# Two-step or three-pass value in the first chunk, weight copies shared out, and an earlier read-back, in a Fourier mixing and GEGLU kernel

## The chip, the cores and the metric

The kernel runs on one core of one Trainium2 chip. The metric is the device time of one execution in microseconds (us); less is better. Nearly all numbers below come from one profiled execution of each kernel, read with the whole program's start as time zero.

TensorE, VectorE, ScalarE and GpSimd are written PE, DVE, ACT and POOL in the profile; PEld is the loading of matmul weights, SP the sync engine that issues most DMAs.

## The reference

```python
X = np.fft.fft(np.fft.fft(x, axis=1), axis=2).real     # x: 8 x 3008 x 256, float32
t = X.reshape(8 * 3008, 256)
g, val = t @ w_gate, t @ w_val                         # 256 x 1536 each
out = (gelu(g) * val) @ w_out                          # 1536 x 256; erf form of gelu
```

## The kernel before

The Fourier transform over the sequence is done by matmuls per batch; the one over the 256 channels is folded into the gate and value weights, which the kernel makes at its start (`make_w`). By symmetry a row and its mirror share an even part E and an odd part O: the gate of a row is E + O, and that of its mirror is E - O with a correction for one channel. The kernel makes a third gate weight "M" (O times -2, one channel set to 0), so that the mirror's gate is a third pass that adds to the same PSUM tile.

The value has no third pass before the change. Its mirror is worked out on VectorE as 2 x VE - V, and the product with the mirror's gelu runs on GpSimd:

```python
def l1_value(ci, fc):
    def run():
        n, c0, E, O, st, fs = cols_of(ci, fc)
        pv = psum("v")
        mm(pv, n, "v", "E", fs, E, True, True)
        ve = ve_tile()
        nc.vector.scalar_tensor_tensor(               # VE: even part plus one channel's term
            ve[:, :n], EB_bufs[b][:, c0 : c0 + n], yw[:, fc : fc + 1], pv[:, :n],
            op0=ALU.mult, op1=ALU.add)
        st["ps"][fc] += [pv, ve]
    return run

def l1_value2(ci, fc):
    def run():
        n, _, _, O, st, fs = cols_of(ci, fc)
        _, gl, pv, ve = st["ps"].pop(fc)
        mm(pv, n, "v", "O", fs, O, False, True, skip_group_check=True)
        nc.vector.tensor_tensor(st["h"][:, fc, 0, :n], gl[:, 0, :n], pv[:, :n], op=ALU.mult)
        vv = v_tile()
        nc.vector.scalar_tensor_tensor(
            _sub(vv, [[-1, n]], n - 1), ve[:, :n], 2.0, pv[:, :n], op0=ALU.mult, op1=ALU.subtract)
        nc.gpsimd.tensor_tensor(st["h"][:, fc, 1, :n], gl[:, 1, :n], vv[:, :n], op=ALU.mult)
    return run
```

Work is laid out in 288 slots, one for each of 12 blocks of 128 features in each of 24 chunks. A slot has a block's gate and value matmuls, the second half of the block before, output matmuls of the chunk before, and "fill" work from a plan:

```python
parts["G"][fc]()                      # gate: E and O passes, first gelu
if before: before[0]["g"][before[1]]()    # third gate pass of the block before, second gelu
parts["V"][fc]()                      # value
...                                   # output matmuls of the chunk before
if before: before[0]["v"][before[1]]()    # value, second part, of the block before
for f in fill.pop(i, []): f()         # weights, transforms of the next batch, ...
```

From the third batch on, the transformed rows S go to DRAM and come back in another layout as Z. The plan puts the two writes (12 and 4 groups of columns) and the read like this, where `s` is the slot of the last transform:

```python
if i == 2: at(fill, s + 1, z_write(b, 0, 12))
if i == 3: at(fill, s + 1, z_write(b, 12, 4))
...
at(fill, s + 3, z_read(b))            # sync engine: Z_sb <- z
...
spread(b, items, s + 7, s0 + NS - 3)  # transposes that read Z_sb, the first at s + 7
```

The stores of the output go through the same sync engine, in program order with these.

Of the kernel before, what the change touches and what calls it, by code (L numbers as in the profile page):

```python
# [28 lines left out]
def kernel(  # L29
# [110 lines left out]
    def psum(tag):  # L140
        bufs = {"g": 2, "v": 3, "o": 1, "dft": 2}[tag]
        return psum_pool.tile([128, 512], FP32, tag=tag, bufs=bufs, name=f"ps_{tag}")
# [283 lines left out]
    def load_wo(q):  # L426
# [3 lines left out]
            in_=ap_replace(  # L430
                moe_w_out, ap=[[C, 128], [128 * C, n], [1, C]], offset=moe_w_out.offset + q * n * 128 * C))

    def make_w(i, f0, n, parts=(0, 1), engine="A", m_at=None, tag="dft"):

        def run():
            ps = psum(tag)
            for k, part in enumerate(parts):
                for half in range(2):
                    nc.tensor.matmul(
                        ps[:, k * n : (k + 1) * n], CW[:, part, half, :], w_raw[:, i, half, f0 : f0 + n],  # L440
                        start=half == 0, stop=half == 1)
            m = n * len(parts)
            dst = _sub(W_sb, [[F, len(parts)], [1, n]], (2 * i + parts[0]) * F + f0)
            if engine == "A":
                nc.scalar.activation(dst, ps[:, :m], AF.Copy)  # L445
            else:
                nc.vector.tensor_copy(dst, ps[:, :m])
            if i == 0 and 1 in parts:
                def minus():
                    nc.scalar.activation(W["g", "M"][:, f0 : f0 + n], ps[:, m - n : m], AF.Copy, scale=keep2)  # L450

                if m_at is None:
                    minus()
                else:
                    m_at.append(minus)
        return run
# [189 lines left out]
    def ffn_work(b):  # L646
        cstate = {}

        def mm(ps, n, nm, part, fs, src, start, stop, **kw):
            nc.tensor.matmul(ps[:, :n], W[nm, part][:, fs], src, start=start, stop=stop, **kw)  # L650

        def cols_of(ci, fc):
            n, c0 = chunk_len[ci], chunk_off[ci]
            E, O = (EO_bufs[b][:, i, c0 : c0 + n] for i in range(2))
            if ci not in cstate:
                cstate[ci] = {"h": h_tile(), "ps": {}, "pso": {}}
            return n, c0, E, O, cstate[ci], slice(fc * 128, (fc + 1) * 128)

        def l1_gate(ci, fc):
            def run():  # L660
                n, _, E, O, st, fs = cols_of(ci, fc)
                pg = psum("g")
                mm(pg, n, "g", "E", fs, E, True, False)
                mm(pg, n, "g", "O", fs, O, False, True)
                gl = gelu_tile()
                nc.scalar.activation(gl[:, 0, :n], pg[:, :n], AF.Gelu)  # L666
                st["ps"][fc] = [pg, gl]
            return run

        def l1_gate2(ci, fc):  # L670
            def run():
                n, _, _, O, st, fs = cols_of(ci, fc)
                pg, gl = st["ps"][fc][:2]
                mm(pg, n, "g", "M", fs, O, False, True, skip_group_check=True)
                nc.scalar.activation(_sub(gl, [[-1, n]], TOK + n - 1), pg[:, :n], AF.Gelu)  # L675
            return run

        def l1_value(ci, fc):
            def run():
                n, c0, E, O, st, fs = cols_of(ci, fc)  # L680
                pv = psum("v")
                mm(pv, n, "v", "E", fs, E, True, True)
                ve = ve_tile()
                nc.vector.scalar_tensor_tensor(  # L684
# [6 lines that stand above are left out]
            def run():  # L691
                n, _, _, O, st, fs = cols_of(ci, fc)
                _, gl, pv, ve = st["ps"].pop(fc)
                mm(pv, n, "v", "O", fs, O, False, True, skip_group_check=True)
                nc.vector.tensor_tensor(st["h"][:, fc, 0, :n], gl[:, 0, :n], pv[:, :n], op=ALU.mult)  # L695
                vv = v_tile()
# [5 lines that stand above are left out]
        def last(ci):  # L702
            return b == B - 1 and ci == NG - 1

        L2P = 4

        def l2_piece(ci, sub, sign, f0):
            def run():
                st = cstate[ci]
                n = chunk_len[ci]  # L710
                m = min(128, n - sub * 128)
                h0 = n - sub * 128 - m if sign else sub * 128
                if last(ci):
                    if f0 == 0:
                        st["pso"][sub, sign] = psum(("o", "g", "v", "dft")[(2 * sub + sign) % 4])
                    pso = st["pso"][sub, sign]
                else:
                    if (sign, f0) == (0, 0):
                        st["pso"][sub] = psum("o")
                    pso = st["pso"][sub]  # L720
                half = slice(sign * C, (sign + 1) * C)
                first = (b, ci, sub) == (0, 0, 0)
                for fc in range(f0, f0 + L2P):
                    nc.tensor.matmul(  # L724
                        pso[:m, half],
                        st["h"][:, fc, sign, h0 : h0 + m],
                        Wo_sb[:, fc, :],
                        start=(fc == 0 and not (first and sign)),
                        stop=(fc == NFC - 1),
                        skip_group_check=first,  # L730
                    )
                if f0 + L2P < NFC:
                    return
                if last(ci):
                    osb = osb_tile()
                    if sign == 0:
                        nc.vector.tensor_copy(osb[:m, 0, :], pso[:m, half])
                        store(b, ci, sub, 0, osb[:, 0, :], nc.sync)
                    else:
                        nc.scalar.activation(osb[:m, 1, :], pso[:m, half], AF.Copy)  # L740
                        store(b, ci, sub, 1, osb[:, 1, :], nc.scalar)
                elif sign == 1:
                    osb = osb_tile()
                    nc.scalar.activation(_sub(osb, [[1, 2 * C]], 0, part_num=m), pso[:m, :], AF.Copy)  # L744
                    store(b, ci, sub, 0, osb[:, 0, :], nc.sync)
                    store(b, ci, sub, 1, osb[:, 1, :], nc.sync)
            return run

        chunks = []
        for ci in range(NG):  # L750
            nsub = (chunk_len[ci] + 127) // 128
            parts = {k: [f(ci, fc) for fc in range(NFC)] for k, f in (
                ("G", l1_gate), ("V", l1_value), ("g", l1_gate2), ("v", l1_value2))}
            subs = [nsub - 1, *range(nsub - 1)] if last(ci) else range(nsub)
            l2s = [l2_piece(ci, s, g, f) for s in subs for g in range(2) for f in range(0, NFC, L2P)]
            chunks.append((parts, l2s))
        return chunks


    def opening():  # L760
# [77 lines left out]
        make_w(0, 0, 256, m_at=minus, tag="o")()  # L838
        ch(0, 0)()
        ch(0, 1, "V")()  # L840
        make_w(1, 0, 256, tag="g")()
        tp_e(0, 0, 0, "V", tag="v")()
        tp_e(0, 0, 1, "A", tag="v")()
        minus[0]()

    def behind_first_gate():
        make_yw(0, 256)()
# [4 lines left out]
    def plan():  # L852
# [7 lines left out]
        for gi in (1, 2):  # L860
            early += [ch(0, 2 * gi), ch(0, 2 * gi + 1, "V"), tp_e(0, gi), tp_o(0, gi, "V"), tp_y(0, gi)]
        for s, f in (
                (0, make_w(0, 256, 256)), (0, make_w(1, 256, 256)), (1, make_yw(256, 256)),
                (1, make_w(1, 512, 512, (1,))), (2, make_w(0, 512, 512, (0,))), (2, make_yw(512, 512)),
                (3, make_w(0, 512, 512, (1,))), (3, make_w(1, 512, 512, (0,))),
                (4, make_w(1, 1024, 512, (1,))), (5, make_w(0, 1024, 512, (0,))), (5, make_yw(1024, 512)),
                (6, make_w(0, 1024, 512, (1,))), (7, make_w(1, 1024, 512, (0,)))):
            at(fill, s, f)
        for i, f in enumerate(early):
            at(fill, (7, 8, 9, 10, 11, 12, 13, 14, 15, 16)[i], f)  # L870
# [31 lines left out]
        for b in range(2, B):  # L902
# [13 lines left out]
            for i, (jg, piece) in enumerate(((2, 1), (1, 2), (0, 3), (3, 4))):  # L916
# [5 lines left out]
                    at(fill, s + 1, z_write(b, 0, 12))  # L922
                if i == 3:
                    at(fill, s + 1, z_write(b, 12, 4))
            at(fill, s + 3, z_read(b))
            items = []
            for gi in range(NG):
                items += [tp_y(b, gi), tp_e(b, gi), tp_o(b, gi)]
# [76 lines left out]
```

## Time and profile before

634.29 us, the median of three runs (633.81 to 635.06).

| reading | before |
| --- | --- |
| span of the profiled run | 631.7 us |
| first gate matmul (end of the opening) | 19.01 us |
| slots 0 to 14 (first to sixteenth gate) | 31.76 us |
| slots 15 to 286 (sixteenth gate to the last slot's) | 563.10 us |
| TensorE's waits on the Z read | 3.4 us, 5 times |

The page gives each engine's busy time, and the chain that ended last, followed back from the last instruction:

```profile
span 631.7 us, 13013 instructions
PE 615.7 (97%) x4276; PEld 406.3 (64%) x4276; DVE 579.5 (92%) x942; ACT 432.9 (69%) x852; POOL 503.3 (80%) x508
PE 84%; DMA 7%; POOL 4%; DVE 2%; issue 1%; ACT 1%; SPq 0%; POOLq 0%; ACTq 0%; DVEq 0%
```

TensorE is busy almost throughout, so only its gaps can be saved. The list of waits, for TensorE's matmuls of the kernel before (what waited, for what, us in total, times, longest), names some of them:

```profile
engine line waited for: us in total, times, longest us
PE ps_dft L602 <- DMA Z_sb<-z: 3.4, 5, 1.1
PE ps_g L650 <- ACT gelu_sb L675: 1.5, 3, 0.7
```

The timeline of TensorE in the kernel before (start, length, engine, line, tiles, shapes, count, and in brackets the idle time before it) shows the gates of slots 0, 4, 5, 8 and 15. The difference of two starts is the length of the slots between:

```profile
19.01 0.82 PE L650 MATMUL ps_g<-EO_sb,W_sb 128*128 128x512 bf16 x2 [0.24 <-DVE EO_sb L584]
...
27.20 1.03 PE L650 MATMUL ps_g<-EO_sb,W_sb 128*128 128x512 bf16 x3
...
29.65 0.81 PE L650 MATMUL ps_g<-EO_sb,W_sb 128*128 128x512 bf16 x3
...
36.35 0.81 PE L650 MATMUL ps_g<-EO_sb,W_sb 128*128 128x512 bf16 x3
...
50.77 0.81 PE L650 MATMUL ps_g<-EO_sb,W_sb 128*128 128x512 bf16 x3
```

Slot 4 takes 2.45 us for matmuls that need about 1.5 (back-to-back 512-column matmuls start 0.217 us apart). Busy time by stretches of the kernel before (stretch, length, then busy us and instructions of each engine) shows who is full there: ScalarE from 20 to 30 us, VectorE and GpSimd from 40 to 50.

```profile
20.00:30.00 10.00, 9.26 (x51) 4.07 (x51) 7.31 (x12) 9.71 (x22) 3.11 (x4) 1.00 1.21 224
40.00:50.00 10.00, 9.57 (x66) 5.48 (x66) 10.00 (x17) 7.61 (x15) 10.00 (x11) 1.00 0.01 2
```

And this is the timeline of the kernel before around one Z read: the write of z, four stores, the read, four stores, and the first matmul that uses Z. (The name SPq marks a DMA's issue by the sync engine; its length is the time the issue takes, not that of the transfer.)

```profile
275.12 0.34 SPq L547 DMA_DIRECT2D z<-S_sb  x1
...
279.12 3.45 SPq L644 DMA_DIRECT2D out_dram<-out_sb  x4
...
282.68 0.52 SPq L558 DMA_DIRECT2D Z_sb<-z  x1
...
284.99 2.38 SPq L644 DMA_DIRECT2D out_dram<-out_sb  x4
...
287.33 0.22 PE L602 MATMUL ps_dft<-TP,Z_sb 128*4 128x128 bf16 x1 [1.05 <-DMA Z_sb<-z]
```

### The profile page before, as it was taken

Reading aid. Unit: us, or ns where it says so; the run is one execution under the profiler, and the core shown is the slowest. Engines: PE = TensorE matmul, PEld = TensorE weight load, DVE = VectorE, ACT = ScalarE, POOL = GpSimd, SP = SyncE. Lnnn points to the kernel's source line nnn. Section 1 sums busy time; section 2 is a strip of 40 time slices with the busy share of each in tenths; the row PEclk is TensorE's granted clock in tenths of the full one; section 3 lists DMA queues with packets and bytes.
Section 4 is the critical chain, followed back from the end, with each engine's and each line's share of the span. In section 5 each row is a group of like instructions: output and inputs, shape, how many; then the busy total and the mean of one; then the engine's idle time right before and its main releaser. Section 6 shows DMA issues by size and latency. Waiting matters only on the chain.

```text
span 631.7 us, 13013 instructions
## 1 busy us (share of the span) xinstructions
PE 615.7 (97%) x4276; PEld 406.3 (64%) x4276; DVE 579.5 (92%) x942; ACT 432.9 (69%) x852; POOL 503.3 (80%) x508
## 2 busy tenths in 40 slices
PE   7899999999999999999999999999999999999997
PEld 3456666666666666665666566666666666666666
DVE  8699889999899989998999999999999999999992
ACT  6887777766777676666766677666676666666661
POOL 8499899989997999878997889969987655555651
PEclk8999999999999999999999999999999999999999
DMA  9941543536363353623644325633222232221123
GB/s 176 230 93 34 141 106 103 146 99 176 84 149 94 102 143 77 179 59 93 156 119 124 107 67 132 147 99 94 61 50 66 70 100 55 52 51 38 43 50 80
DMA packets 52505, 63.83 MB, mean 101 GB/s; under 512 B 7783, under 2 KB 48218, under 8 KB 50042
## 3 DMA queue, kind: packets, MB, share of 16 engines
q1 hardware_dynamic: 45238, 47.23, 29.0%
q0 software_dynamic: 6608, 15.29, 11.2%
q8 instruction: 33, 0.54, 0.4%
q10 hardware_dynamic: 592, 0.49, 0.3%
q14 instruction: 34, 0.28, 0.2%
HBM read 38.86 MB, written 29.38 MB: 108 GB/s over the span
## 4 chain that ended last, share of the span: by engine, by line
PE 84%; DMA 7%; POOL 4%; DVE 2%; issue 1%; ACT 1%; SPq 0%; POOLq 0%; ACTq 0%; DVEq 0%
PE ps_o L724 35%; PE ps_g L650 26%; PE ps_v L650 17%; DMA Z_sb<-z 4%; DMA w_raw<-in_moe_w_gate_dram 2%; POOL h_sb L699 2%; PE ps_dft L536 2%; PE ps_dft L572 1%; DVE v_sb L697 1%; POOL xb L158 1%; DMA EO_sb<-yrow 1%; POOL w_raw L422 1%; PE ps_dft L602 1%; PE ps_dft L517 1%; PE ps_g L724 0%
## 5 line engine op out<-in xcount | busy, mean ns | idle before, releaser
L699 POOL TENSOR_TENSOR h_sb<-gelu_sb,v_sb 128x512 bf16<-128x512 bf16 (+1 forms) x288 | 328.8, 1145 | 101.4 <-DVE v_sb L697 95.9
L724 PE MATMUL ps_o<-Wo_sb,h_sb 128*128 128x256 bf16 (+1 forms) x2232 | 334.8, 273 | 0.4 <-POOL h_sb L699 0.4
L724 PEld LDWEIGHTS <-h_sb 128*128 128x128 bf16 (+1 forms) x2304 | 228.8, 100 | 112.1 <-POOL h_sb L699 1.9
L684 DVE SCALAR_TENSOR_TENSOR ve_sb<-EB_sb,yw,ps_v 128x512 f32<-128x512 bf16 (+1 forms) x288 | 212.3, 737 | 34.0 <-PE ps_v L650 29.4
L666 ACT ACTIVATE gelu_sb<-ps_g 128x512 bf16<-128x512 f32 (+1 forms) x288 | 169.6, 589 | 96.9 <-PE ps_g L650 94.8
L650 PE MATMUL ps_g<-EO_sb,W_sb 128*128 128x512 bf16 (+1 forms) x864 | 231.0, 375 | 2.0 <-ACT gelu_sb L675 1.5
L650 PE MATMUL ps_v<-EO_sb,W_sb 128*128 128x512 bf16 (+1 forms) x576 | 214.0, 375 | 0.5 <-ACT W_sb L445 0.5
L695 DVE TENSOR_TENSOR h_sb<-gelu_sb,ps_v 128x512 bf16<-128x512 bf16 (+1 forms) x288 | 195.3, 678 | 1.3 <-ACT gelu_sb L675 1.0
L697 DVE SCALAR_TENSOR_TENSOR v_sb<-ve_sb,ps_v 128x512 f32<-128x512 f32 (+1 forms) x288 | 192.9, 670 | 0.0
L650 PEld LDWEIGHTS <-W_sb 128*128 128x128 bf16 x1440 | 136.7, 98 | 81.9 <-issue 3.3
L675 ACT ACTIVATE gelu_sb<-ps_g 128x512 bf16<-128x512 f32 (+1 forms) x288 | 169.1, 587 | 0.0
L744 ACT ACTIVATE out_sb<-ps_o 128x512 f32<-128x512 f32 x92 | 54.9, 597 | 34.8 <-PE ps_o L724 34.7
L223 POOL TENSOR_TENSOR eo_sb<-ab_sb 94x512 bf16<-94x512 f32 (+1 forms) x60 | 66.6, 1111 | 0.1
L582 ACT ACTIVATE EO_sb<-ps_dft 128x512 bf16<-128x512 f32 (+1 forms) x44 | 26.0, 590 | 22.9 <-PE ps_dft L572 20.7
L539 ACT ACTIVATE S_sb<-ps_dft 96x512 bf16<-96x512 f32 x48 | 28.2, 587 | 11.3 <-PE ps_dft L536 11.3
L216 POOL TENSOR_TENSOR ab_sb<-x_raw,x_raw 94x508 f32<-94x508 f32 (+1 forms) x30 | 32.9, 1098 | 0.0
L219 POOL TENSOR_TENSOR ab_sb<-x_raw,x_raw 94x508 f32<-94x508 f32 (+1 forms) x30 | 32.9, 1097 | 0.0
L536 PE MATMUL ps_dft<-eo_sb,G 94*96 94x256 bf16 x102 | 19.2, 274 | 0.0
L158 POOL DMA_INDIRECT x_raw<-in_x_dram,idx x18 | 17.0, 942 | 2.8 <-issue 0.8
L572 PE MATMUL ps_dft<-TP,Z_sb 128*128 128x128 bf16 (+1 forms) x184 | 17.9, 218 | 0.4 <-DVE Z_sb L524 0.4
L572 PEld LDWEIGHTS <-Z_sb 128*128 128x128 bf16 x192 | 14.6, 98 | 2.4 <-DVE Z_sb L524 0.9
L158 POOL DMA_INDIRECT xb<-in_x_dram,idx x8 | 7.7, 965 | 9.2 <-DMA w_raw<-in_moe_w_val_dram 4.1
(140 smaller groups left out, 170.4 us busy)
## 6 DMA issues: line engine op xcount, KB each, us to landing
out_dram<-out_sb SPq DMA_DIRECT2D x361, 64.0 KB
x_raw<-in_x_dram SPq DMA_DIRECT2D x10, 768.0 KB
Z_sb<-z SPq DMA_DIRECT2D x6, 768.0 KB
z<-S_sb SPq DMA_DIRECT2D x6, 576.0 KB
EB_sb<-yrow SPq DMA_DIRECT2D x14, 128.0 KB
x_raw<-in_x_dram SPq DMA_DIRECT2D x2, 640.0 KB
z<-S_sb SPq DMA_DIRECT2D x6, 192.0 KB
EB_sb<-yrow SPq DMA_DIRECT2D x7, 120.2 KB
```

Source lines behind the costliest of these rows:

```text
L216: eng.tensor_tensor(ab(0, 1, up), fwd(1, up), mir(255, down), op=ALU.add)
L223: eng.tensor_tensor(_sub(eo, [[C, nj], [1, 128]], j0 * C + g * 128), ab(0, 0, [[1, 128]]), ab(1, 0, [[1, 128]]), op=op)
L572: nc.tensor.matmul(ps[:, o : o + n], st["Z"][:, pair, g * 128 : g * 128 + 128], _sub(TP, [[1, n]], g * 128), start=True, stop=True)
L650: nc.tensor.matmul(ps[:, :n], W[nm, part][:, fs], src, start=start, stop=stop, **kw)
L666: nc.scalar.activation(gl[:, 0, :n], pg[:, :n], AF.Gelu)
L675: nc.scalar.activation(_sub(gl, [[-1, n]], TOK + n - 1), pg[:, :n], AF.Gelu)
L684: nc.vector.scalar_tensor_tensor(ve[:, :n], EB_bufs[b][:, c0 : c0 + n], yw[:, fc : fc + 1], pv[:, :n], op0=ALU.mult, op1=ALU.add)
L695: nc.vector.tensor_tensor(st["h"][:, fc, 0, :n], gl[:, 0, :n], pv[:, :n], op=ALU.mult)
L697: nc.vector.scalar_tensor_tensor(_sub(vv, [[-1, n]], n - 1), ve[:, :n], 2.0, pv[:, :n], op0=ALU.mult, op1=ALU.subtract)
L699: nc.gpsimd.tensor_tensor(st["h"][:, fc, 1, :n], gl[:, 1, :n], vv[:, :n], op=ALU.mult)
L724: nc.tensor.matmul(pso[:m, half], st["h"][:, fc, sign, h0 : h0 + m], Wo_sb[:, fc, :], start=(fc == 0 and not (first and sign)), stop=(fc = ...
L744: nc.scalar.activation(_sub(osb, [[1, 2 * C]], 0, part_num=m), pso[:m, :], AF.Copy)
```

## The change

The intent has three parts. (1) For the first eight blocks of the first chunk the value gets a third pass as the gate has it, so VectorE needs two products where it needed a sum, a product and another sum, and GpSimd, still busy issuing loads, needs no product. (2) The copies of the new weights out of PSUM, all on ScalarE before, are dealt out between ScalarE and VectorE. (3) The Z read stands one slot earlier.

```diff
     def make_w(i, f0, n, parts=(0, 1), engine="A", m_at=None, tag="dft"):
...
-            if i == 0 and 1 in parts:
+            if 1 in parts and (i == 0 or f0 < V3_TO):              # V3_TO = 1024
                 def minus():
-                    nc.scalar.activation(W["g", "M"][:, f0 : f0 + n], ps[:, m - n : m], AF.Copy, scale=keep2)
+                    if i and f0 == 0:
+                        W["v", "M"] = work([128, V3_TO], BF16, "osb", 3, "w_minus")[:, :]
+                    dst, src = W["gv"[i], "M"][:, f0 : f0 + n], ps[:, m - n : m]
+                    if engine == "A":
+                        nc.scalar.activation(dst, src, AF.Copy, scale=keep2)
+                    else:
+                        nc.vector.tensor_scalar(dst, src, keep2, None, op0=ALU.mult)
...
+        def three(ci, fc):
+            return b == 0 and ci == 0 and fc * 128 < V3_TO
...  l1_value:
+                if three(ci, fc):
+                    gl = st["ps"][fc][1]
+                    mm(pv, n, "v", "E", fs, E, True, False)
+                    mm(pv, n, "v", "O", fs, O, False, True)
+                    nc.vector.tensor_tensor(st["h"][:, fc, 0, :n], gl[:, 0, :n], pv[:, :n], op=ALU.mult)
+                    st["ps"][fc] += [pv, None]
+                    return
...  l1_value2:
+                if three(ci, fc):
+                    mm(pv, n, "v", "M", fs, O, False, True, skip_group_check=True)
+                    nc.vector.tensor_tensor(
+                        st["h"][:, fc, 1, :n], gl[:, 1, :n], _sub(pv, [[-1, n]], n - 1), op=ALU.mult)
+                    return
...  opening:
-        make_w(1, 0, 256, tag="g")()
+        make_w(1, 0, 256, m_at=minus, tag="g")()
...
         minus[0]()
+        minus[1]()
...  plan, (slot, weights):
-                (0, make_w(0, 256, 256)), (0, make_w(1, 256, 256)), (1, make_yw(256, 256)),
-                (1, make_w(1, 512, 512, (1,))), (2, make_w(0, 512, 512, (0,))), (2, make_yw(512, 512)),
-                (3, make_w(0, 512, 512, (1,))), (3, make_w(1, 512, 512, (0,))),
-                (4, make_w(1, 1024, 512, (1,))), (5, make_w(0, 1024, 512, (0,))), (5, make_yw(1024, 512)),
-                (6, make_w(0, 1024, 512, (1,))), (7, make_w(1, 1024, 512, (0,)))):
+                (0, make_w(0, 256, 256)), (0, make_w(1, 256, 256, engine="V")), (1, make_yw(256, 256)),
+                (1, make_w(1, 512, 512, (1,))), (2, make_w(0, 512, 512, (0,), "V")), (2, make_yw(512, 512)),
+                (3, make_w(0, 512, 512, (1,))), (3, make_w(1, 512, 512, (0,), "V")),
+                (4, make_w(1, 1024, 512, (1,), "V")), (5, make_w(0, 1024, 512, (0,), "V")), (5, make_yw(1024, 512)),
+                (6, make_w(0, 1024, 512, (1,))), (7, make_w(1, 1024, 512, (0,), "V"))):
...
-            at(fill, s + 3, z_read(b))
+            at(fill, s + 2, z_read(b))
```

More of the change, by code (lines that the diff above doesn't have):

```diff
@@ L431, in load_wo @@
                 moe_w_out, ap=[[C, 128], [128 * C, n], [1, C]], offset=moe_w_out.offset + q * n * 128 * C))
+    V3_TO = 1024
     def make_w(i, f0, n, parts=(0, 1), engine="A", m_at=None, tag="dft"):
```

## The prediction

> What bounds it now. The page shows TensorE busy 615.7 of 631.7 us (97%), and the chain that ended last is 84% TensorE. Only TensorE's gaps can be saved. The list of waits and the timeline put them in two places.
>
> (a) First chunk. Counting slots from each group of gate matmuls, slots 0 to 14 run from 19.0 to 50.8 us. Back-to-back 512-column matmuls start 0.217 us apart, 256-column ones 0.109. A slot's matmuls at these rates against its length leave, by my estimate, 4 to 5 us of gaps: 0.6 in slot 1 (weight load, evacuation), 0.9 in slot 4 (ScalarE's evacuations; ScalarE is busy 9.71 of 10 us at 20 to 30 us), 0.6 in slot 5 (gelu buffers held by late GpSimd products), the rest in slots 8 to 14. There VectorE runs without a break from 37.4 us, so those gaps are VectorE's.
>
> (b) The Z read-back. In five of six batches the first transposes wait for it: TensorE 3.4 us, weight loads 4.8 us. In one case the read is issued at 282.68, behind four stores that wait for ScalarE until 279.12; its first user starts at 287.33.
>
> What the change does.
> - Adds eight 512-column matmuls, 8 x 0.217 = 1.7 us of TensorE, in slots 1 to 8.
> - Removes eight VectorE sums (0.66 us start to start) and turns eight others (0.60) into products: -5.3 us. It moves five evacuations and one half-size one with its scaling to VectorE: about +4. VectorE no longer waits 2.1 us for EB before its first product.
> - Takes eight products of 1.14 us from GpSimd, whose backlog starts at 29.7 us, behind its DMA issues.
> - ScalarE loses six evacuations (about 3 us) and gains about 1 us of scalings, one of them ahead of the first gelu.
> - The sync queue's order now has the read directly behind its write in five of six batches. The second keeps stores between; it did not wait before.
>
> The Trainium skill, "DMA: Bandwidth & Descriptors" ("Two DMAs through the same engine are not ordered"), says that a dependent DMA must wait for the first one's completion. So the read will wait for the write, but should still start some 4 us earlier, more than the longest wait of 1.3 us. "VectorE: DVE Perf Modes" ("Why PSUM operands drop a tier") excludes the two-port mode for PSUM operands; the trace agrees (sum, product and copy out of PSUM all 0.60 to 0.66 us), so a reversed product should cost 0.60.
>
> On the critical path. Slots 2 and 3 are dense, so added matmuls lengthen them; the gaps of slots 4 and 5 pay that back. Slot 8 should start about 0.25 us before 36.35. From there VectorE still bounds slots 8 to 14 with unchanged blocks, starting a little earlier with one operation less queued. Gain of the first chunk: about 1.0 us (0 to 2). Z read: about 3.6 us (2 to 4.5). TensorE is dense elsewhere.
>
> Predicted: 634.3 - 4.6 = 629.7 us, range 627.3 to 632.2. Chances: faster by over 2% 0.01, within 2% 0.98, slower by over 2% 0.01.
>
> Right if: the waits on the Z read vanish; slot 15's gate starts near 49.8 instead of 50.77 us; VectorE stays near 100% at 40 to 50 us; reversed products take 0.60.
>
> Wrong if: the read, blocked by its write, delays stores and output buffers; extra scalings delay the first gelu; evacuations queued behind VectorE's products hold the weight PSUM buffers; or slots 8 to 14 shrink by 2 us because GpSimd bound them.

## The result, and the profile after

The changed kernel takes 630.64 us (median of four runs, 629.61 to 631.59) against 634.67 us for the kernel before (four runs, 633.81 to 635.38). The ratio is 0.9937, with a 95% interval of 0.9916 to 0.9958. Ratios here are the mean time of one kernel's fast runs over that of the other's of the same rounds, so not quite the ratio of the medians that are quoted.

| stretch of the profiled run, us | before | after | difference |
| --- | --- | --- | --- |
| opening, to the first gate | 19.01 | 19.81 | +0.80 |
| slots 0 to 14 | 31.76 | 32.37 | +0.61 |
| slots 15 to 286 | 563.10 | 559.31 | -3.79 |
| the rest | 17.81 | 17.51 | -0.3 |
| span | 631.7 | 629.0 | -2.7 |

(The last two rows are what is left of the spans; the other rows are differences of gate starts in the timelines.)

The opening varies by chance: over the fourteen profiles the first gate starts between 18.26 and 19.81 us in ten and between 20.6 and 20.8 in four, two runs of the changed kernel differ by 0.46 us, and four kernels whose opening has the very same code (before, z_only, z_early_act and deal_only) start at 19.01, 18.97, 20.61 and 20.73. The four late ones are all among the seven kernels without the third pass, so a small effect of the change on the opening is not excluded.

The other two rows repeat for the changed kernel: its second profile gives 32.37 and 559.12. For the kernel before there is one profile, but z_only, pad8, pad128 and turn_buffers below leave its first chunk as it is and take 32.00, 31.24, 31.76 and 31.23 us. So the loss of the first chunk is 0.4 to 1.1 us, by which of them one takes; its sign holds against each. The last row's -0.3 stands in every profile with the third pass except gate3's, and its cause was not looked for. So the total was forecast well, but the first chunk got longer, not shorter, and nearly all of the gain lies behind it.

The page of the kernel after, engines and chain:

```profile
span 629.0 us, 12958 instructions
PE 616.1 (98%) x4235; PEld 408.3 (65%) x4284; DVE 578.3 (92%) x941; ACT 430.7 (68%) x848; POOL 494.5 (79%) x500
PE 91%; DVE 2%; ACT 2%; issue 2%; POOL 1%; DMA 1%; POOLq 0%; DVEq 0%; ACTq 0%
```

DMA falls from 7% to 1% of the chain. The wait on the Z read is gone from TensorE's list in the kernel after, and a wait on VectorE's weight copies is new:

```profile
engine line waited for: us in total, times, longest us
...
PE ps_g L659 <- ACT gelu_sb L684: 1.0, 3, 0.4
PE ps_dft L581 <- DVE Z_sb L533: 0.7, 2, 0.5
PE ps_v L659 <- DVE W_sb L450: 0.4, 1, 0.4
```

TensorE's timeline in the kernel after: the gates of slots 0, 3, 4, 5, 8 and 15, with a value matmul in slot 8 and a transpose in slot 14 that wait for VectorE. (Line numbers move with the added lines: L650 of before is L659 here, L602 is L611, L644 is L653.)

```profile
19.81 0.82 PE L659 MATMUL ps_g<-EO_sb,W_sb 128*128 128x512 bf16 x2 [0.24 <-DVE EO_sb L593]
...
26.60 0.81 PE L659 MATMUL ps_g<-EO_sb,W_sb 128*128 128x512 bf16 x3 [0.33 <-ACT gelu_sb L684]
...
28.76 1.03 PE L659 MATMUL ps_g<-EO_sb,W_sb 128*128 128x512 bf16 x3
...
30.98 0.81 PE L659 MATMUL ps_g<-EO_sb,W_sb 128*128 128x512 bf16 x2
...
37.77 0.81 PE L659 MATMUL ps_g<-EO_sb,W_sb 128*128 128x512 bf16 x3
39.00 0.39 PE L659 MATMUL ps_v<-EO_sb,W_sb 128*128 128x512 bf16 x1 [0.42 <-DVE W_sb L450]
...
51.90 0.27 PE L581 MATMUL ps_dft<-TP,Z_sb 128*128 128x128 bf16 x2 [0.53 <-DVE Z_sb L533]
...
52.18 0.81 PE L659 MATMUL ps_g<-EO_sb,W_sb 128*128 128x512 bf16 x3
```

The same two stretches of the kernel after: ScalarE has room from 20 to 30 us, GpSimd from 40 to 50; VectorE is still full there.

```profile
20.00:30.00 10.00, 9.40 (x53) 4.28 (x53) 6.79 (x11) 8.77 (x21) 2.23 (x3) 1.00 1.20 232
40.00:50.00 10.00, 9.59 (x66) 5.50 (x66) 10.00 (x18) 7.23 (x14) 6.28 (x7) 1.00 0.01 2
```

And the Z read of the same batch in the timeline of the kernel after:

```profile
276.32 0.34 SPq L556 DMA_DIRECT2D z<-S_sb  x1
...
279.47 0.34 SPq L567 DMA_DIRECT2D Z_sb<-z  x1
...
280.33 8.25 SPq L653 DMA_DIRECT2D out_dram<-out_sb  x8
...
287.42 0.22 PE L611 MATMUL ps_dft<-TP,Z_sb 128*4 128x128 bf16 x1
```

The read now goes 3.2 us after the write was issued, ahead of the eight stores, and its first user waits for nothing. The sync engine's own list of waits shows that the read (L567) does wait for its write, in five of the six batches:

```profile
SPq L567 <- DMA z<-S_sb: 13.1, 5, 2.9
```

The stores are not hurt: their first group starts at 280.33.

### The profile page after: what moved, and what is told of

Its sections match the earlier page's. It is cut to its first block, busy times and chain, and to the rows that moved or that the text cites. A ratio compares the mean times of both kernels' runs of the same rounds, so it can differ in the third digit from the quotient of the medians.

```text
span 629.0 us, 12958 instructions
## 1 busy us (share of the span) xinstructions
PE 616.1 (98%) x4235; PEld 408.3 (65%) x4284; DVE 578.3 (92%) x941; ACT 430.7 (68%) x848; POOL 494.5 (79%) x500
## 4 chain that ended last, share of the span: by engine, by line
PE 91%; DVE 2%; ACT 2%; issue 2%; POOL 1%; DMA 1%; POOLq 0%; DVEq 0%; ACTq 0%
PE ps_o L748 37%; PE ps_g L659 28%; PE ps_v L659 19%; PE ps_dft L545 2%; PE ps_dft L581 1%; POOL h_sb L723 1%; PE ps_o L819 1%; PE ps_dft L526 1%; DMA EO_sb<-yrow 1%; ACT gelu_sb L675 1%; PE ps_dft L442 1%; PE ps_dft L611 0%; PE ps_g L748 0%; ACT gelu_sb L684 0%; PE ps_v L389 0%
## 5 line engine op out<-in xcount | busy, mean ns | idle before, releaser
L723 POOL TENSOR_TENSOR h_sb<-gelu_sb,v_sb 128x512 bf16<-128x512 bf16 (+1 forms) x280 | 319.6, 1144 | 102.0 <-DVE v_sb L721 93.7
L659 PE MATMUL ps_g<-EO_sb,W_sb 128*128 128x512 bf16 (+1 forms) x816 | 228.3, 375 | 4.0 <-ACT gelu_sb L684 1.0
L703 DVE SCALAR_TENSOR_TENSOR ve_sb<-EB_sb,yw,ps_v 128x512 f32<-128x512 bf16 (+1 forms) x280 | 206.2, 736 | 26.9 <-PE ps_v L659 25.7
L659 PE MATMUL ps_v<-EO_sb,W_sb 128*128 128x512 bf16 (+1 forms) x575 | 213.7, 375 | 0.6 <-DVE W_sb L450 0.4
L719 DVE TENSOR_TENSOR h_sb<-gelu_sb,ps_v 128x512 bf16<-128x512 bf16 (+1 forms) x280 | 189.7, 677 | 1.1 <-ACT gelu_sb L684 0.7
L659 PEld LDWEIGHTS <-W_sb 128*128 128x128 bf16 x1440 | 136.7, 98 | 81.3 <-issue 2.0
L721 DVE SCALAR_TENSOR_TENSOR v_sb<-ve_sb,ps_v 128x512 f32<-128x512 f32 (+1 forms) x280 | 187.2, 669 | 0.0
```

The source lines that it names most:

```text
L659: nc.tensor.matmul(ps[:, :n], W[nm, part][:, fs], src, start=start, stop=stop, **kw)
L703: nc.vector.scalar_tensor_tensor(ve[:, :n], EB_bufs[b][:, c0 : c0 + n], yw[:, fc : fc + 1], pv[:, :n], op0=ALU.mult, op1=ALU.add)
L721: nc.vector.scalar_tensor_tensor(_sub(vv, [[-1, n]], n - 1), ve[:, :n], 2.0, pv[:, :n], op0=ALU.mult, op1=ALU.subtract)
```

## The experiments

Two theories stood at the start. A: the earlier read is the whole gain, and the first-chunk parts cost a little. B: the gain is shared, as predicted, about 1 us of it from the first chunk. The runs below first split the change.

In all that follows, "chunk" is the length of slots 0 to 14, and "batches" that from the sixteenth gate to the last slot's gate, both from the profiled run; before has 31.76 and 563.10. The waits in the last column are those of matmuls; weight loads are counted apart.

| run | edit, from | time, us (runs) | before in the same rounds | ratio (95%) | chunk | batches | TensorE's waits on the Z read |
| --- | --- | --- | --- | --- | --- | --- | --- |
| z_only | read sooner; before | 630.78 (6) | 634.63 (11) | 0.9947 (0.9928 to 0.9965) | 32.00 | 559.29 | none |
| chunk_only | read put back; after | 631.19 (6) | 634.63 (11) | 0.9959 (0.9940 to 0.9978) | 32.37 | 560.07 | none |
| three_only | third pass alone; before | 631.31 (4) | 634.63 (11) | 0.9963 (0.9937 to 0.9989) | 32.60 | 559.22 | none |
| deal_only | dealt copies alone; before | 637.59 (4) | 634.63 (11) | 1.0052 (1.0027 to 1.0078) | 33.82 | 563.38 | 4.0 |
| pad8 | 8 tiny matmuls; before | 631.42 (4) | 632.63 (9) | 0.9967 (0.9949 to 0.9984) | 31.24 | 559.88 | none |
| pad128 | 128 tiny matmuls; before | 633.42 (1) | 632.63 (9) | one run | 31.76 | 562.43 | 3.3 |
| turn_buffers | buffer turn; before | 635.48 (1) | 632.63 (9) | one run | 31.23 | 563.92 | 4.1 |
| all_moves | three moves; after | 630.46 (5) | 632.63 (9) | 0.9960 (0.9946 to 0.9973) | 31.38 | 559.86 | none |
| after_again | none; after | 630.18 (6) | 633.27 (11) | 0.9952 (0.9935 to 0.9970) | 32.37 | 559.12 | none |
| all_moves_again | three moves; after | 629.76 (6) | 633.27 (11) | 0.9949 (0.9929 to 0.9970) | 31.38 | 559.21 | none |
| z_early_act | see below; before | 631.31 (6) | 633.27 (11) | 0.9980 (0.9952 to 1.0008) | 30.57 | 559.31 | none |
| gate3 | PSUM buffers; all_moves | 740.26 (1) | 633.27 (11) | one run | | | |

All results were correct. The single runs of pad128, turn_buffers and gate3: their traces are used for what waits, not for the time.

### z_only

```diff
-            at(fill, s + 3, z_read(b))
+            at(fill, s + 2, z_read(b))
```

> The kernel before with nothing but the Z read a slot sooner. Theory A (the read-back is the whole gain, the first chunk costs a little): TensorE's waits on the Z read, 3.4 us, vanish and the time falls by 3.8 us (3.2 to 4.4), ratio about 0.994; within the trace, gate to gate times change only at the batches that waited (about -0.3, -1.1, -0.9, -0.5, -0.8 us). Rival B (the gain is shared as predicted, about 1 us from the first chunk): the time falls by 3.0 us or less, ratio 0.9955 or more.

Measured: the waits vanish, and from the sixteenth gate on the profile is 3.81 us shorter; slot times change at the batches that had waited, by -1.13, -0.95, -0.52 and -0.83 us. (The first, by -0.35; but that one also shows in runs whose other waits stayed, so it is chance.) The ratio stands for 3.4 us. This is what A expects. But A fell with the next run.

### chunk_only

```diff
-            at(fill, s + 2, z_read(b))
+            at(fill, s + 3, z_read(b))
```

> The changed kernel with the Z read put back to its old slot: first-chunk changes alone. Theory A: from the first gate to the sixteenth takes 32.4 us, 0.6 longer than before's 31.76, and the time is 0.3 to 1.0 us longer than before (ratio 1.0005 to 1.0016); the waits on the Z read stay near 3.4 us. Rival B: that stretch is 1 us shorter in most runs and the changed kernel's profile was an outlier; ratio about 0.9985. If the opening before the first gate is 0.8 us longer here too, the opening shift belongs to the change; if it is 19.0 us as before, it was chance.

Measured: slots 0 to 14 take 32.37 us, as A says. But the kernel is 2.6 us faster than before by its ratio, where A said slower, and the waits on the Z read are gone, although the read stands where it stood. The batches take 560.07 us: 3.03 of the 3.8 us come without the earlier read. B is no better off, since the gain is not in the first chunk. A new theory was needed, one that explains how a change in the first 40 us takes away waits at 287, 362, 437 and 511 us.

### three_only

```diff
-                (0, make_w(0, 256, 256)), (0, make_w(1, 256, 256, engine="V")), ...   # and five more with "V"
+                (0, make_w(0, 256, 256)), (0, make_w(1, 256, 256)), ...               # all on ScalarE, as in before
-            at(fill, s + 2, z_read(b))
+            at(fill, s + 3, z_read(b))
```

> Before with the value of the first eight blocks in three passes, but all weight evacuations (and the new scalings) left on ScalarE, Z read in the old slot. Theory A: ScalarE, already busy 9.7 of 10 us at 20 to 30 us, gets about 1.6 us more to do, so the first 16 gates take longer than with the dealing: 33 to 34 us against 32.4, and time 1 to 2 us over before. Rival B (GpSimd's late products were the real limit of the first chunk): 31.5 us or less even so.

Measured: the third pass alone costs 0.84 us in the first chunk (32.60), less than expected. And the time is 3.3 us under before by the medians (2.3 by the ratio), not 1 to 2 over: it too takes the Z waits away.

### deal_only

```diff
-   (the plan's weights with everything on ScalarE)
+   (0, make_w(0, 256, 256)), (0, make_w(1, 256, 256, engine="V")), ...   # the changed kernel's six with "V"
```

> Before with only the weight evacuations dealt to VectorE, value in two passes, Z read in the old slot. Theory A: the ScalarE gap of slot 4 (0.9 us) shrinks but VectorE gets 6 x 0.6 = 3.6 us more work in a stretch that it already fills from 29 us on, so the first 16 gates take 32.5 to 34.5 us; time 0.7 to 2.5 us over before. Rival: the dealing alone closes slot 4's gap and saves 0.5 to 1 us, the three passes being what costs.

Measured: 2.06 us lost in the first chunk, as theory A expected: VectorE's copies now stand behind its own two-step blocks. (The time is 3.3 us over before by the ratio, more than the 0.7 to 2.5 expected; this run's profile has one of the late openings, 20.73 us.) TensorE's list of waits in this kernel:

```profile
PE ps_dft L602 <- DMA Z_sb<-z: 4.0, 4, 1.4
PE ps_v L650 <- DVE W_sb L447: 2.5, 2, 1.3
```

Here the Z waits stay. So the dealing pays only together with the third pass, where it turns a loss of 0.84 into one of 0.61. And the thing that takes the Z waits away is in the third pass.

### pad8, pad128 and turn_buffers: why the Z read came late

A look at single DMA issues gave theory C. Of the four stores ahead of the read in the kernel before, one takes 1.63 us to issue, the others 0.48 to 0.60. In the same moment a 16 KB packet of an instruction queue is under way. Below: the issue times of stores from 279 to 289 us (min/median/max ns), and the DMA queues from 279.0 to 282.8 us (packets, MB, share), both of the kernel before:

```profile
L644 SPq DMA_DIRECT2D out_dram<-out_sb x8: 466/589/1633, 279.1 to 286.8; - x8
...
q1 hardware_dynamic: 202, 0.17, 19.1%
q8 instruction: 1, 0.02, 2.3%
q14 instruction: 1, 0.01, 0.9%
```

The queue q8 has 33 packets of 16 KB in the whole run. The Trainium skill, "Runtime: NRT & Kernel Launch" ("Instruction fetch mechanics"), says that a sequencer fetches its own instructions over a DMA queue in 16 KiB blocks of 256 instructions, at a cost that is "mostly hidden". 33 packets are then 8,448 instructions, an estimate that fits TensorE alone: its 4,276 matmuls and 4,276 weight loads. A batch in mid-run has 512 matmuls (36 blocks with 5 of gate and value and 8 of output each, 17 of the transform, 27 of the transposes), each with its weight load: 1,024 instructions, exactly four packets. So a fetch that falls on the stores ahead of one read does so in every batch: in the kernel before, fetches start at 205.30, 280.16, 355.61, 430.01 and 504.68 us, each 1.9 to 2.5 us ahead of a read. (The batch at 205 us does not feel it, since its first transpose comes later, and the one at 144 us has no fetch; it waits only 0.28 us.) In the other four, what the slow store took over 0.59 us is 1.04, 0.81, 0.52 and 0.70 us, and TensorE's waits there are 1.05, 0.87, 0.46 and 0.75. The third pass adds eight matmuls, 16 instructions, early in the stream, and moves every later fetch. The traces of the two runs that had to be explained agree: in chunk_only and three_only these fetches come 4.1 to 4.4 us ahead of the reads, and no store of the four ahead of a read takes over 0.60 us.

The test adds the 16 instructions and nothing else:

```diff
+        def pad(n):
+            ps = psum("o")
+            for _ in range(n):
+                nc.tensor.matmul(ps[0:1, 0:1], idle[:, 0:1], idle[:, 0:1], start=True, stop=True)
...
         warm(6)
+        pad(8)
```

> Before, its Z read in the old slot, with eight 1x1 matmuls added in TensorE's idle time of the opening: 16 more instructions in TensorE's stream, as the first-chunk change has, and nothing else. Theory C (the read is late because a 16 KB instruction fetch of TensorE's stream, which comes at the same place of every batch, falls on the four stores ahead of it; the 16 instructions move the fetch away): the fetches beside the reads come about 2.4 us sooner, no store ahead of a read takes over 1 us, TensorE's waits on the Z read fall from 3.4 us to under 0.5, the time by 3 us or more. Rival D (something else of the first-chunk change, such as its extra tile among the output buffers, or chance): waits of 3 to 4 us stay and the time is as before.

Measured: TensorE's matmuls wait no more, its weight loads 1.3 us instead of 4.8; the batches take 559.88 us (-3.2), and the kernel is faster than before (ratio 0.9967) although it does only more. The ratio stands for 2.1 us, less than the 3 us expected; the opening of this profile is one of the late ones (20.73 us). The fetches come at 203.85, 278.71, 352.87, 426.56 and 500.60 us, 3.9 to 4.4 us ahead of the reads, so 1.6 to 2.1 us sooner against them than before (about 2.4 was expected). Timeline, store issues and DMA queues in the same windows of pad8:

```profile
280.27 2.41 SPq L644 DMA_DIRECT2D out_dram<-out_sb  x4
...
282.79 0.52 SPq L558 DMA_DIRECT2D Z_sb<-z  x1
...
287.36 0.22 PE L602 MATMUL ps_dft<-TP,Z_sb 128*4 128x128 bf16 x1
...
L644 SPq DMA_DIRECT2D out_dram<-out_sb x8: 467/592/599, 280.3 to 287.9; - x8
...
q1 hardware_dynamic: 181, 0.15, 15.8%
q14 instruction: 1, 0.01, 0.5%
```

The four stores take 2.41 us where they took 3.45, and no q8 packet is among them; of all stores ahead of the six reads none takes over 0.60 us. The absolute times hardly differ from those of before, because here everything runs about 1.1 us behind: the write is at 276.26 instead of 275.12. Counted from its write, the read is issued 6.5 us later instead of 7.6. The first user of Z still comes 4.6 us after the read, but has no more to wait.

pad128 is the same with `pad(128)`, one whole packet.

> The same with 128 tiny matmuls, 256 instructions: one whole 16 KB fetch (64 bytes for an instruction, an estimate from 33 fetches of 16 KB for some 8,500 instructions). Theory C: the fetches fall where they fell in the kernel before, so at least four of the reads again have a fetch on the stores ahead of them and TensorE's waits on the Z read are 2.5 to 4.5 us; the opening is some us longer. Rival (any shift, or the longer opening, takes the waits away): under 0.5 us of waits.

Measured: the waits are back, and q8 has 34 packets, one more than the 33 of every other profile. The fetches at the reads come at 205.31, 280.00, 354.85, 429.82 and 504.90 us, within 0.8 us of where they came before. TensorE's list of waits, the timeline and the store issues of pad128, with the q8 packet among the stores again:

```profile
PE ps_dft L602 <- DMA Z_sb<-z: 3.3, 4, 1.2
...
278.96 3.31 SPq L644 DMA_DIRECT2D out_dram<-out_sb  x4
...
286.96 0.22 PE L602 MATMUL ps_dft<-TP,Z_sb 128*4 128x128 bf16 x1 [0.83 <-DMA Z_sb<-z]
...
L644 SPq DMA_DIRECT2D out_dram<-out_sb x8: 467/589/1488, 279.0 to 286.6; - x8
...
q8 instruction: 1, 0.02, 2.1%
```

The opening did not get longer by some us, as was expected: TensorE was idle there, and the first gate starts at 19.65 us.

The third pass also takes one of the three output buffers for its weight, which shifts their turn. turn_buffers does that alone:

```diff
         minus[0]()
+        nc.vector.memset(osb_tile()[0:1, 0, 0:1], 0.0)
```

> Before with one unused tile taken once from the three output buffers, so that their turn is shifted as the first-chunk change shifts it, and no TensorE instruction more. Theory C: waits on the Z read stay at 3 to 4.5 us and the time is as before. Rival D: they vanish.

Measured: 4.1 us of waits, so the buffers are not the cause. The one time, 635.48 us, is above before's, with an opening of 20.74 us. Theory C stands: 16 instructions in TensorE's stream take the waits away, 256 bring back the fetch and the waits, the buffer turn does nothing. How regular it is can be counted. Over all fourteen profiles, behind the opening, 117 stores follow another DMA's issue within 0.15 us and begin while a q8 packet is under way; 110 of them take over 0.8 us. Of the 3,796 such stores that begin outside the packets, 53 do. The first store of a group is spared: 57 began inside a packet and none took over 0.8 us. So what it takes is a fetch that falls on a run of back-to-back issues. What inside the DMA engines or the sync engine makes those issues slow, no run shows.

### all_moves, z_early_act and gate3: the first chunk

The first chunk of the changed kernel has three gaps with a name: slot 2 (gate after ScalarE's late gelu), slot 8 (value after VectorE's copy of the last weights), and slots 8 to 14, which the prediction put down to VectorE. all_moves edits the changed kernel for all three (a gate's wait counts in the slot before it, since slots are counted from gate to gate):

```diff
-  early += [ch(0, 2 * gi), ch(0, 2 * gi + 1, "V"), tp_e(0, gi), tp_o(0, gi, "V"), tp_y(0, gi)]
+  early += [ch(0, 2 * gi), ch(0, 2 * gi + 1), tp_e(0, gi), tp_o(0, gi), tp_y(0, gi)]
-  (1, make_w(1, 512, 512, (1,))), ... (7, make_w(1, 1024, 512, (0,), "V"))
+  (1, make_w(1, 512, 512, (1,), "V")), ... (7, make_w(1, 1024, 512, (0,)))
```

> The changed kernel with three moves: the last odd value weights' first evacuation (and its scaling) to VectorE, the last evacuation back to ScalarE, and the first batch's later Z and EO evacuations from VectorE to ScalarE. If VectorE bounds slots 8 to 14 and the waits in slots 2 and 8 are the evacuations': slot 2 loses 0.3 us, slot 8 0.4 us, slots 9 to 14 together 0.6 to 1.6 us; first to sixteenth gate 30.0 to 31.2 us against 32.4, time 1 to 2.4 us under the changed kernel (ratio to before 0.9905 +- 0.0015). Rival (GpSimd or TensorE bounds slots 9 to 14): these stay as they are, 32 us or more in all.

Measured: chunk 31.38 us, 1.0 under the changed kernel, just above the range expected, with slots 9 to 14 together 0.64 us shorter, at the low end of theirs; the ratio to before, 0.9960, is well above the 0.9905 expected. Slot 2 falls from 2.40 to 2.15 us, slot 8 from 2.11 to 1.88, slot 14 from 2.60 to 2.04. But slots 9 to 12 stay (1.77, 2.15, 1.78, 1.80) and slot 13 gives 0.08 (2.12), though VectorE has four copies less. So behind slot 8, VectorE's queue made slot 14's gap and little more. What TensorE meets at the gate of slot 9 in all_moves is this:

```profile
39.09 0.59 PE L659 MATMUL ps_g<-EO_sb,W_sb 128*128 128x512 bf16 x2 [0.20 <-ACT gelu_sb L684]
```

The gate waits for the second gelu of the block two before it, which has to free one of the two PSUM buffers of the gate. The gate of slot 10 does the same for 0.30 us. gate3 takes a third buffer for the gate from the value:

```diff
-        bufs = {"g": 2, "v": 3, "o": 1, "dft": 2}[tag]
+        bufs = {"g": 3, "v": 2, "o": 1, "dft": 2}[tag]
```

> The three-move version with three PSUM buffers for the gate and two for the value, instead of two and three. If the thin slots 9, 11 and 12 (1.77 to 1.80 us, with about 1.5 us of matmuls in 9 and 12) are held by the loop gate, two gelus, next gate but one, over two buffers, slots 9 and 12 fall below 1.70 us and TensorE no longer waits there for ScalarE's second gelu; if they are held by VectorE or by ScalarE's own work they stay at 1.77 or more. Two value buffers may bring new waits on VectorE, which would show by name.

Measured: 740.26 us. With two value buffers TensorE waits 61.0 us for VectorE in 170 places, beginning in slot 9. Slot 8 does fall from 1.88 to 1.52 us, but slot 9 is 1.74, with a wait of 0.27 us for VectorE in it. So the run fits the two-buffer loop in slot 8 and settles nothing for the others; it stays open. It does show that giving up the third value buffer costs some 110 us.

z_early_act goes without the third pass: the kernel before with the read a slot sooner and the first edit of all_moves.

> Before with only the Z read a slot sooner and the first batch's later Z and EO evacuations moved from VectorE to ScalarE; no third pass. Theory: slot 14's wait for VectorE (0.5 us) goes, slots 0 to 8 stay as before; first to sixteenth gate 31.1 to 31.5 us, no waits on the Z read, time as good as the version with three moves (within 0.5 us). Rival (the third pass is worth its 1.7 us of TensorE): 0.5 us or more slower than that version.

Measured: slot 14 falls from 2.61 to 2.04 us, so the four copies alone made that gap. Its first chunk is the shortest, 30.57 us, below the range, but 0.5 of that comes from where its opening ended. Slot 5 takes 1.83 us in four of the profiles without the third pass (pad8, pad128, turn_buffers, z_early_act) and 2.36 and 2.60 in before and z_only. (The seventh, deal_only, has 2.39 without this wait.) In before and z_only a gelu waits 0.52 and 0.76 us for GpSimd's first product, and the next gate waits for ScalarE. GpSimd, which issues loads until then, starts that product at 29.3 to 30.0 us in all of these, wherever the first gate is: 10.7 and 10.9 us behind the first gate in before and z_only, whose openings are short, and 8.7 to 10.3 us in the four. With 2.36 in slot 5 the chunk would be 31.1. Its times do not bear the promise out: five of six runs lie at 630.88 to 631.52 and one at 635.92, against 630.18 for the changed kernel in the same rounds. Against the version with three moves (629.76, below) it is 1.55 us slower by the medians, as the rival said; but in the traces its chunk and batches are together 0.7 us shorter, and the loss is in the late opening (first gate at 20.61 us) and in an end 1.4 us longer than that of before. Neither was followed up, so the rival is not shown by this.

> The changed kernel again, unedited, on the same chip as the next two. First to sixteenth gate 32.4 us, no waits on the Z read, ratio to before 0.994 to 0.996 by what its trace shows (3.8 us of waits gone, 0.6 us lost in the first chunk).

> The version with the three moves again, beside the changed kernel: first to sixteenth gate 31.4 us, 1.0 us less than the changed kernel's 32.4, so 0.5 to 1.5 us faster than it in the same rounds, unless the opening's chance hides it.

Measured: the changed kernel's trace repeats to within 0.2 us (32.37 and 559.12), and so does that of all_moves (31.38 and 559.21). The version is 1.0 us shorter in the trace, and 0.4 us by the medians of the same rounds (629.76 against 630.18). That is within the scatter of single runs and below the 0.5 us expected, so no version is shown to beat the changed kernel by the clock.

## Why the prediction was right or wrong

**The time.** 629.7 us was predicted, a fall of 4.6 us; the fall by the medians is 4.0 us (630.64 against 634.67), inside the range and within the 2% that was forecast. This is not because each term held.

**The Z read: right in size and in its cure, incomplete in its cause.** "About 3.6 us (2 to 4.5)" against 3.79 in the trace of the changed kernel and 3.81 in z_only. The read starts earlier behind its write, no stores are hurt, no waits are left. The read waits for its write, as the Trainium skill ("DMA: Bandwidth & Descriptors", "Two DMAs through the same engine are not ordered") demands: it is issued 3.2 us after the write was, and the sync engine waits for the write 13.1 us in five batches. What the prediction missed is why the read was late by just so much. It blamed the stores that wait for ScalarE. They do stand in front, but in pad8 they still do, and nothing waits. The 0.5 to 1.0 us that hurt came from an instruction fetch on top of them, and the third pass moves that fetch by its mere 16 instructions. So two parts of the change each cure the same wait, and their gains do not add: 3.4 us for the one, 2.6 for the other (its own loss included), 4.0 and 3.0 for both in the two sets of rounds (each from its ratio).

**The first chunk: wrong in sign.** The step that failed is "Gain of the first chunk: about 1.0 us (0 to 2)"; measured is a loss of 0.61 us (0.4 to 1.1 against the other profiles of the unchanged first chunk). Of its own tests, VectorE did stay full and the products did take 0.60 us, but slot 15's gate starts at 52.18 us (51.73 in the second profile) and not near 49.8. It fails in two terms.

- "The gaps of slots 4 and 5 pay that back", with slot 8 to start 0.25 us sooner. Counted from the first gate, slot 8 starts 0.62 us later (17.96 against 17.34), and slot 8 itself is 0.15 us longer, with its value's wait of 0.42 us for VectorE's copy of the last weights. The eight passes cost 8 x 0.217 = 1.74 us. After taking 0.217 off each of slots 0 to 7, slots 1, 4 and 5 give back 0.49, 0.45 and 0.57 us. (Slot 5 could give that back only because this profile of before has a short opening, as told under z_early_act; from a slot of 1.83 us it would be 0.04.) Slot 2 takes 0.39 more: the gelu that frees the gate's PSUM buffer is late behind a scaling that the third pass put on ScalarE, 0.57 us from its start to the next one's. all_moves moves it to VectorE and 0.25 us comes back. The prediction named this danger only for the first gelu. Slot 4 keeps half its gap, since its first value weights are now copied by VectorE behind two products. (The passes are in slots 0 to 7, not 1 to 8, as the changed source shows.)
- "VectorE still bounds slots 8 to 14 ..., starting a little earlier with one operation less queued". VectorE is indeed full from 40 to 50 us, but being busy is not being waited for. Slots 9 to 14 together changed by 0.16 us, and with four copies less on VectorE only slot 14 moved by more than 0.1 us (by 0.56, all_moves). At the gates of slots 9 and 10 of that version TensorE waits for ScalarE's second gelu. For the lighter slots the two gate buffers are the likely limit, which gate3 did not settle.

**Right on the way.** A product out of PSUM with the reversed operand costs what the others cost: in the profile after, VectorE's operations in the eight blocks start 0.60 us apart. "VectorE: DVE Perf Modes" ("Why PSUM operands drop a tier") rules out the two-port mode for any operand in PSUM, and the trace has no faster product. GpSimd's products did not hold slots 9 to 14: in the kernel after GpSimd is busy 6.28 of 10 us from 40 to 50 us instead of 10.00, and none of these slots got shorter by more than 0.06 us. In slot 14 of before TensorE does wait 0.41 us for one of them; with GpSimd relieved the slot is as long as it was (2.60 against 2.61), since there VectorE's copy holds it next (0.53 us). In slot 5 of before they did cost 0.5 us, as the prediction said.

## What to carry to other kernels

When a DMA in a steady loop is late by the same bit each time round, look at the issue time of each DMA ahead of it: a group of stores that takes 3.4 us once and 2.4 us elsewhere is a lead, and an instruction fetch may sit on it. Then a change that adds or drops a few instructions of another engine can move waits far behind it, so split a change into its parts, and try a harmless padding, before crediting a part with what its run gained. And a full engine is no bound by itself: take some of its work away and see whether the slots get shorter.

## What the Trainium skill lacked or had wrong

- "Runtime: NRT & Kernel Launch" ("Instruction fetch mechanics") has the blocks right: 16 KB packets, 33 of them for 8,552 TensorE instructions, 34 with pad128's 256 more, which bring the fetches back to their old places. But it counts the cost of a boundary as mostly hidden. TensorE's own stream was not seen to stall on it here, yet the sync engine did: in the kernel before, 16 of the 21 sync DMAs behind the opening whose issue took over 0.8 us (against 0.59) began while such a packet was under way, where only 3 other stores began, and through the Z read this cost TensorE about 3 us.
- "DMA: Bandwidth & Descriptors" does not say that these fetches can slow the issue of data DMAs, from 0.59 to 1.63 us in the case shown, nor does any page that was read.
- No page that was read says that the phase of the fetches follows the number of instructions ahead, so that a loop of a whole number of blocks (here 1,024 instructions a batch, about 75 us) meets them at the same place each time: 16 instructions more took 3.2 us off the batches, 256 more 0.7.
